# Routing attention followed by a cosine router: first pair prepared in another order, placing steps moved ahead of turns, POOL additions ordered behind DVE additions, scatters split in two

## The chip, the cores and the metric

The kernel runs on one core of a Trainium2 chip. The metric is the device time of one execution in microseconds (us), as the median of several runs. TensorE is called PE here, VectorE DVE, ScalarE ACT, GpSimd POOL and SyncE SP, as the profile calls them.

## The reference

There are two blocks, one behind the other. The first is attention in 4 batches and 8 heads over 768 tokens of 64 numbers. A query sees only the keys that have the same nearest centroid (of 16 in each head). The second block sends each of the 3072 tokens to one of 8 experts.

```python
q_assign = np.argmax(np.einsum('bhsd,hcd->bhsc', q_n, c_n), axis=-1)   # q_n, k_n, c_n: unit rows
k_assign = np.argmax(np.einsum('bhsd,hcd->bhsc', k_n, c_n), axis=-1)
mask = q_assign[:, :, :, None] == k_assign[:, :, None, :]
scores = np.where(mask, scale * (q @ k.T), -1e9)
attn_out = softmax(scores) @ v                      # then (B,H,S,D) -> x of (3072, 512)
logits = (x_n @ emb_n.T) / tau                      # 8 experts
e, gate = argmax(logits), its softmax probability
out[token] = gate * (relu(x[token] @ w1[e]) @ w2[e])     # w1: 512x1024, w2: 1024x512, all float32
```

## The kernel before

All five engines are scheduled by hand (`tc.manual_schedule`): the order of the calls in the Python source is the order of the instructions in the queue of each engine. So a call that is moved in the source is moved in the queues of all the engines that it gives work to. The places and names below are those that the change and the prediction use.

**Attention, 16 pairs.** The work is cut into pairs n of two heads (4 batches of 4 pairs). A pair has two halves of queries (hq 0 and 1) with 6 key blocks each, so 12 units. The main loop takes two units in one turn, so a pair has six turns, it = 0 to 5. In each turn PE computes the scores of two units that come two units later (`scores`, L512: a bfloat16 product with a one-hot table "hot" that adds the mask, and the float32 product of qT and kT), ACT takes the exponential (`expo`, L523, into one of six buffers prob), and PE multiplies two older units by v (`attend`, L534, sum o_ps). DVE adds the probabilities of all blocks of a half into acc (L543 for the first two blocks, L553 for each of the others). Behind the last block of a half ACT copies o_ps to o_sb (L558), and `unite` adds its two parts into o_sum (L567), on POOL for all pairs but the last. `total` (it 0 of the next pair) sums acc over the partitions on PE (L581), DVE turns and inverts the sums (L598, L599), POOL spreads them (L602), `divide` (it 2) applies them (L613, L617), and `rows` turns the result (L634) and writes it to x_rows in memory.

**Preparing a pair.** `turn0` and `turn1` transpose q and k of a pair. From pair 1 on this is done by DVE (L395, one instruction for each), two pairs ahead, in turns 4 and 5. qT and kT have two buffers, so the turn of pair n + 2 has to wait until PE has read those of pair n. For pair 0 PE transposes in halves (L378) and ACT or DVE copies (L384, L386). `products` multiplies with the centroids cnB (PE, L405; DVE turns the result, L414), `choose` finds the nearest centroid (DVE, L423 to L426), `codes` writes its code to cd (ACT, L431, L444), and SP transposes cd by DMA into hot (L449). For pairs from 2 on, products come in turn 0, choose in turn 1 and codes in turn 2 of the pair before. For pair 1 they come in turns 1, 2 and 3.

**begin()** issues the first loads and makes constants. `unit_centroids` scales the centroids (L249, L250, L302), transposes them (L304) and copies them into cnB (L307). It stands between the turns of q and of k. `unit_experts` (L249, L250, L314, L315) is the last call; `turned_experts` (PE L320, DVE L323) comes in turn 2 of pair 0.

**Routing beside the attention.** For three of the four batches the expert choice (`route_pieces`) and the placing of the tokens into blocks (`Places`, table `early`) are DVE, POOL and small PE steps, put into turns of pairs 4 to 15. In the code before, the turns of q and k (it 4 and 5) stand inside `between`, ahead of the route steps and of the table `early`.

**Experts.** After the attention come 4 early items and then 16 items in `later`: block, sized, sized, block, sized, block, ..., sized, block. A block has 128 tokens, a sized item 160 to 272 of one expert. `fetch` gathers rows of x with indirect DMAs from POOL (L1069), `hidden` / `sized_hidden` and `result` / `sized_result` are the two products (L1289, L1305, L1204, L1241), and `send` scatters the pieces of a sized item with 5 to 9 indirect DMAs from POOL (L1080). A block's single scatter (also L1080) stands in `result`. Weights are loaded by SP (L1119).

Of the kernel before, what the change touches and what calls it, by code (L numbers as in the profile page):

```python
# [39 lines left out]
def kernel(  # L40
# [38 lines left out]
    NB = NS + KX  # L79


    MORE = (2, 4, 8)
    NO = sum(MORE)
    assert -(-(N - P - min(CAPS)) // P) <= KX + NO and min(CAPS) >= P
# [92 lines left out]
    def misc():  # L177
        return bank("misc", psM)
# [50 lines left out]
    def keep_up(n, bk):  # L229

        for _ in range(n):
            nc.tensor.matmul(
                bk.rearrange("p (g x) -> p g x", x=P),
                lhsT=onesb,
                rhs=bc(onesb, [P, 4, P], 1),
                start=True,
                stop=True,
            )
# [88 lines left out]
    def begin():  # L327

        nc.scalar.dma_start(out=c_sb, in_=centroids.rearrange("h c d -> (h c) d"))
        load(0, "q")  # L330
        load(0, "k")
        load(0, "v")
        load(1, "qk")
        constants()

        nc.scalar.activation(en_r, epsc[0:E], ACTF.Sqrt)
        norm_rows(cn_r, c_sb, P)
        nc.scalar.dma_start(out=emb, in_=moe_expert_emb)
        nc.scalar.dma_start(out=tau, in_=moe_tau.to_broadcast([E, 1]))
        piece(0, "turn0")  # L340
        unit_centroids()
        piece(0, "turn1")
        norm_rows(en_r, emb, E)

        nc.scalar.activation(cn_r, epsc, ACTF.Exp)
        piece(0, "products")
        for m in range(2):
            scores(m, (1,))
        un[2]["s_ps"] = psO.tile([P, 2, 512], F32, tag="o_ps", name="s_ps2")
        scores(2, (1,))  # L350
        piece(0, "choose")
        piece(0, "codes")
        keep_up(6, misc())
        rest = piece(0, "turn_numbers")
        next(rest)
        for m in range(3):
            scores(m, (0,))
        for m in (0, 2, 1):
            expo(m)
        next(rest, None)  # L360
        token_numbers()
        unit_experts()

    def prep_pieces(n):

# [7 lines left out]
        def turn(nm, half):  # L373
            if half == 0:
                t[nm + "T"] = trp.tile([P, S], F32, tag=nm + "T", name=nm + "T")
            bk = misc() if nm == "k" else idle_ps[:, half]
            for j in range(NJ // 2):
                nc.tensor.transpose(  # L378
                    bk[:, P * j : P * j + P],
                    t[nm][:, NJ // 2 * half + j].rearrange("p h d -> p (h d)"),  # L380
                    ident,
                )
            if nm == "q":
                nc.scalar.copy(t["qT"][:, HS * half : HS * half + HS], bk[:, 0:HS])  # L384
            else:
                (nc.scalar.copy if half else nc.vector.tensor_copy)(  # L386
                    in_halves(t["kT"])[:, half], bk[:, 0:HS].rearrange("p (s t) -> p s t", t=SQ)
                )
# [171 lines left out]
    def unite(g):  # L560

        n, hq, _ = units[GU * g]
        t = ld[n]
        if hq == 0:
            t["o_sum"] = xp.tile([P, 2, HE], F32, tag="o_sum", name="o_sum", bufs=2)
        add = (nc.gpsimd if n + 1 < NP else nc.vector).tensor_tensor
        add(t["o_sum"][:, hq], t["o_sb"][:, 0], t["o_sb"][:, 1], ALU.add)  # L567

# [551 lines left out]
            out=w[:, c], in_=x[ds(e, 1)].rearrange("o (c p) f -> p (o c) f", p=P)[:, c]  # L1120
        )

    def fetch(it):
        mo[it] = {}
        if it.kind == "sized":
            u0, n = FIRST[it.j], WIDE[it.j]
            xs = mo[it]["xs"] = szp.tile([P, max(WIDE), P], F32, tag="xs", name="xs")
            for u in range(n):
                gather(xs[:, u], x_pieces, flat(gpidx)[:, u0 + u : u0 + u + 1], NQ * N)
            return  # L1130
        if it.kind == "whole":
            xin = mo[it]["xin"] = it.xin
            gather(
                xin.rearrange("p w x -> p (w x)"), x_rows, it.tables[1][:, it.col : it.col + 1], N
            )
            return
        xin = mo[it]["xin"] = xip.tile([P, NQ, P], F32, tag="xin", name="xin")
        if it.kind == "early":
            n = SA * P
            gather(  # L1140
                xin.rearrange("p w x -> p (w x)"), x_rows[0:n], gidxs[0][:, it.j : it.j + 1], n
            )
            return
        for w in range(NQ):
            gather(xin[:, w], x_pieces, it.tables[0][:, it.col, w : w + 1], NQ * N)
# [119 lines left out]
            ys[:, 0:n], ys[:, 0:n], bc(flat(gates4)[:, u0 : u0 + n], [P, n, P], 2), ALU.mult  # L1265
        )

    def send(it):

        u0 = FIRST[it.j]  # L1270
        for u in range(WIDE[it.j]):
            at = flat(spidx)[:, u0 + u : u0 + u + 1]
            scatter(out_pieces, at, mo[it]["ys"][:, u], NQ * N)
        del mo[it]

    def flat(t):
        return t.rearrange("p k w -> p (k w)")
# [80 lines left out]
    def between(n, it):  # L1358
        b, nb = divmod(n, NHP)
        if n == 0:  # L1360

            if it == 0:
                piece(1, "turn0")
                piece(1, "turn1")
            elif it == 2:
                piece(1, "choose")
                turned_experts()
            elif it == 3:
                later_constants()
        elif it == 0 and n > 1:  # L1370
            rows(2 * n - 4, 2 * n - 3)
        elif it == 1:
            piece(n + 1, "choose")
        elif it == 3 and n == NP - 1:
            rows(2 * n - 2, 2 * n - 1)
        if it == 4:
            piece(n + 2, "turn0")
        elif it == 5:
            piece(n + 2, "turn1")
        if b > 0:  # L1380
            if nb == 0 and it == 3:
                route[b - 1] = route_pieces(b - 1)
            products, logits, read, norms, choose = route.get(b - 1, (None,) * 5)


            m = NJ * nb + it
            if m in (8, 11, 14):
                read((m - 8) // 3 * 2, (m - 8) // 3 * 2 + 2)
            if m in (15, 16, 18, 19, 21, 22):
                norms((15, 16, 18, 19, 21, 22).index(m))  # L1390
            if (nb, it) == (0, 5):
                logits(0, 1)
            elif (nb, it) == (1, 4):
# [14 lines left out]
        if (n, it) in first:  # L1408
            w, j, i = first[n, it]
            own = E0[j]  # L1410
            if own.e is None:
                own.e = expert_of(own)
            x, chunks = (moe_w1, KD) if w is w1s else (moe_w2, KF)
            load_part(w[own.slot], x, own.e, chunks, i, 2)
# [9 lines left out]
    with tc.manual_schedule(engines=by_hand):  # L1424
        begin()
        for i in range(0, len(units), 2):
# [8 lines left out]
            for m in range(i + 2 if i else 3, min(i + 4, len(units))):  # L1435
                scores(m)
                expo(m)
                if it == (2 if n else 3) and m == i + 2:
                    piece(n + 1, "codes")
            between(n, it)  # L1440
            if it == 4 and n == NP - 1:
# [1 line left out]
            b, nb = divmod(n, NHP)  # L1443
            if (b, nb, it) in early:
                early[b, nb, it]()
            if i + 2 == len(units):
                ats.close()
                tile_waits = {"side": "right", "reuse_waits": "tile"}
                psX = ctx.enter_context(tc.tile_pool(name="psX", bufs=1, space=PSUM, **tile_waits))
                turn_x(E0[0], nc.scalar.copy, xp.tile([P, DM], F32, tag="acc", name="xTm", bufs=3))  # L1450
# [10 lines left out]
                route[b][0](0)  # L1461
            if it == 0 and n > 0:
                total(2 * n - 2, 2 * n - 1)
            if it == (0 if n else 1):
                piece(n + 1, "products")
            if (nb, it) == (0, 4) and b > 0:
                route[b - 1][0](0, 1)
# [70 lines left out]
        pb.hot_gates(NB)  # L1538
        hidden(E0[3])
        weights1(later[1])  # L1540
        fetch(later[1])
        result(E0[2])
        weights2(later[0])
        turn_x(later[0])
        result(E0[3])
# [35 lines left out]
                        more(MORE[0] + MORE[1], MORE[2])  # L1581

        LAST = len(later) - 1
        for i, it in enumerate(later):
            if i == LAST - 1:
                overflow()
# [5 lines left out]
                turn_x(later[i + 1])  # L1592
            if i > 0 and i + 2 < len(later) and later[i + 2].kind == "sized":
                fetch(later[i + 2])
            if i > 0 and later[i - 1].kind == "sized":
                send(later[i - 1])
                if i == LAST:
                    nc.gpsimd.drain()
            if it.kind == "sized":
                sized_hidden(it)  # L1600
            else:
                hidden(it)
            if i == 0:
                pb.gates(slot_gates)
            for j in range(i + 2, min(i + 4, len(later))):
# [62 lines left out]
```

## Time and profile before

| what | value |
|---|---|
| median of 3 runs | 706.15 us (706.08 to 707.62) |
| the profiled execution, its own time | 701.07 us |
| its span, first to last instruction | 699.3 us |
| granted PE clock over the span | 0.999 |
| busy time PE / DVE / ACT / POOL | 686.4 / 385.6 / 263.3 / 253.0 us |
| attention ends, experts begin (on PE) | about 331 us |
| first product with v (L534) of pair 0 | 16.52 us |

The span is what the trace shows; the profiled execution's own time has 1.8 us around it. The profiled execution was 5.1 us shorter than the median of the runs without a profile. In the profile a line "idle before <- releaser" tells how long an engine stood and what ended the wait. Busy PE time is modelled and overlaps between matmuls, so the pace of PE is better read from the distance of equal points in the loop, such as the first L534 of each turn.

### The profile page before, as it was taken

The page shows a single profiled execution, that of the slowest core. Times are in us where ns is not written, and L with a number is a line of the kernel's source. Part 1 is how long each engine was busy: PE and PEld are TensorE (multiplying, and loading weights), DVE is VectorE, ACT ScalarE, POOL GpSimd, SP SyncE. Part 2 cuts the span into 40 slices and gives each one's busy share as a digit, 9 for nine tenths or more (in the row PEclk, how much of TensorE's full clock was granted, in tenths as well). Part 3 has the DMA queues.
Part 4 walks back from the last instruction along what each step waited for, and adds up shares of the span by engine and source line. Part 5 has one row for each costly group of instructions (what it writes and reads, how often), then busy time and mean ns, then how long its engine had stood idle before and what let it go on. Part 6 is the DMA issues. An engine that isn't in the chain of part 4 may idle for free.

```text
span 699.3 us, 16130 instructions
## 1 busy us (share of the span) xinstructions
PE 686.4 (98%) x6517; PEld 461.2 (66%) x6517; DVE 385.6 (55%) x666; ACT 263.3 (38%) x444; POOL 253.0 (36%) x403
## 2 busy tenths in 40 slices
PE   8999999999999999999999999999999999999996
PEld 3544444444444444454966678897979797979694
DVE  5878988998989999999583121240220303030310
ACT  5556564677566765576315110101010111111111
POOL 2122221311133212354214456736264554635402
PEclk9999999999999999999999999999999999999999
DMA  9755567775677678699799978258768686879450
GB/s 135 106 98 100 101 97 96 150 142 106 109 132 151 104 150 155 170 249 256 172 318 355 349 271 281 90 216 290 260 228 301 207 302 233 307 250 323 141 221 32
DMA packets 244156, 135.55 MB, mean 194 GB/s; under 512 B 207840, under 2 KB 207842, under 8 KB 244076
## 3 DMA queue, kind: packets, MB, share of 16 engines
q1 hardware_dynamic: 237084, 121.08, 65.5%
q0 software_dynamic: 6016, 13.12, 5.3%
q8 instruction: 54, 0.88, 0.6%
q10 hardware_dynamic: 976, 0.25, 0.2%
q14 instruction: 26, 0.21, 0.1%
HBM read 115.92 MB, written 13.12 MB: 185 GB/s over the span
## 4 chain that ended last, share of the span: by engine, by line
PE 76%; DVE 7%; issue 6%; DMA 6%; POOL 2%; SPq 1%; ACT 1%; POOLq 0%; DVEq 0%; ACTq 0%
PE s_ps L512 16%; PE o_ps L534 12%; PE h_ps L1289 10%; PE y_ps L1305 10%; PE h_ps L1204 9%; PE y_ps L1241 5%; PE misc L1241 5%; DVE acc L553 3%; DMA out_dram<-ys,spidx 3%; PE x_ps L1204 3%; PE misc L581 2%; PE misc L405 1%; DMA q<-in_q_dram 1%; SPq L212 1%; DMA w1s<-in_moe_w_dram 1%
## 5 line engine op out<-in xcount | busy, mean ns | idle before, releaser
L523 ACT ACTIVATE prob<-s_ps 128x768 f32<-128x768 f32 x192 | 154.2, 814 | 105.4 <-PE s_ps L512 104.4
L512 PE MATMUL s_ps<-qT,kT 64*64 64x384 f32 x1536 | 155.9, 482 | 0.0
L534 PE MATMUL o_ps<-prob,v 64*64 64x385 f32 x1536 | 141.7, 484 | 0.0
L553 DVE TENSOR_TENSOR acc<-acc,prob 128x768 f32<-128x768 f32 x128 | 127.3, 995 | 8.8 <-ACT prob L523 0.5
L534 PEld LDWEIGHTS o_ps<-prob,v 64*64 64x64 f32 x1536 | 59.5, 133 | 63.8 <-issue 56.3
L1250 DVE STREAM_TRANSPOSE ys<-y_ps 128x256 f32<-128x256 f32 (+4 forms) x16 | 6.7, 417 | 153.2 <-PE y_ps L1241 153.2
L567 POOL TENSOR_TENSOR o_sum<-o_sb 128x385 f32<-128x385 f32 x30 | 30.6, 1021 | 161.8 <-ACT o_sb L558 161.8
L1289 PE MATMUL h_ps<-xTm,w1s 128*128 128x128 f32 x768 | 88.3, 275 | 0.0
L1289 PEld LDWEIGHTS h_ps<-xTm,w1s 128*128 128x128 f32 x768 | 87.4, 192 | 1.4 <-issue 1.0
L1305 PE MATMUL y_ps<-w2s,hT 128*128 128x512 f32 x192 | 84.5, 593 | 0.0
L1080 POOL DMA_INDIRECT out_dram<-ys,spidx x56 | 56.5, 1009 | 74.7 <-DVE ys L1264 59.8
L512 PEld LDWEIGHTS s_ps<-qT,kT 64*64 64x64 f32 x1536 | 55.8, 133 | 36.1 <-issue 32.0
L1204 PE MATMUL h_ps<-xTs,w1s 128*128 128x272 f32 (+7 forms) x384 | 72.9, 346 | 1.1 <-ACTq L1565 1.1
L1204 PEld LDWEIGHTS h_ps<-xTs,w1s 128*128 128x128 f32 x384 | 66.6, 190 | 8.0 <-issue 2.4
L1296 ACT ACTIVATE hT<-h_ps 128x512 f32<-128x512 f32 x24 | 14.3, 596 | 144.3 <-PE h_ps L1289 144.3
L512 PE MATMUL s_ps<-hot 64*64 64x384 bf16 x768 | 64.8, 326 | 2.1 <-DMA hot<-cd 0.9
L1069 POOL DMA_INDIRECT xs<-x_rows,gpidx x56 | 57.3, 1023 | 17.1 <-issue 16.8
L1305 PEld LDWEIGHTS y_ps<-w2s,hT 128*128 128x128 f32 x192 | 35.6, 190 | 40.2 <-issue 40.2
L512 PEld LDWEIGHTS <-hot 64*64 64x64 bf16 x768 | 24.3, 106 | 45.6 <-issue 41.9
L602 POOL COPY inv<-inv 32x12 f32<-32x12 f32 x120 | 31.2, 260 | 50.0 <-DVE inv L599 45.6
L1241 PE MATMUL y_ps<-hTs,w2o 128*128 128x272 f32 (+7 forms) x256 | 48.0, 346 | 0.0
L1241 PE MATMUL misc<-hTs,w2o 128*128 128x272 f32 (+7 forms) x256 | 48.0, 346 | 0.0
(270 smaller groups left out, 687.2 us busy)
## 6 DMA issues: line engine op xcount, KB each, us to landing
w1s<-in_moe_w_dram SPq DMA_DIRECT2D x18, 2048.0 KB, 8.3
w2s<-in_moe_w_dram SPq DMA_DIRECT2D x18, 2048.0 KB, 13.2
v<-in_v_dram SPq DMA_DIRECT2D x128, 48.0 KB, 2.4
k<-in_k_dram SPq DMA_DIRECT2D x62, 96.0 KB, 3.6
q<-in_q_dram SPq DMA_DIRECT2D x60, 96.0 KB, 3.6
x_rows<-xb SPq DMA_DIRECT2D x60, 96.0 KB, 2.7
xr<-x_rows SPq DMA_DIRECT2D x9, 512.0 KB, 4.8
w1s<-in_moe_w_dram SPq DMA_DIRECT2D x4, 1024.0 KB, 5.7
```

Source lines behind the costliest of these rows:

```text
L512: nc.tensor.matmul(s_ps[D * half : D * half + D, h, 0:HS], lhsT=l[rows, half], rhs=r[rows], start=part == (1 if len(parts) < 2 else 0), st ...
L523: nc.scalar.activation(d["prob"][:, :, 0:HS], d["s_ps"][:, :, 0:HS], ACTF.Exp, scale=scale)
L534: nc.tensor.matmul(g["o_ps"][D * h : D * h + D, half, 0:HE], lhsT=ld[n]["v"][keys, j, h], rhs=d["prob"][keys, h, 0:HE], start=(j == 0), st ...
L553: nc.vector.tensor_tensor(g["acc"], g["acc"], d["prob"][:, :, 0:HS], ALU.add)
L567: add(t["o_sum"][:, hq], t["o_sb"][:, 0], t["o_sb"][:, 1], ALU.add)
L602: nc.gpsimd.tensor_copy(inv2[M * to : M * to + M, :, i % 2], inv[M * i : M * i + M])
L1069: nc.gpsimd.indirect_dma_start(out=to, out_offset=None, in_=of, in_offset=bass.IndirectOffsetOnAxis(ap=at, axis=0), bounds_check=n - 1, oo ...
L1080: inst = nc.gpsimd.indirect_dma_start(out=to, out_offset=bass.IndirectOffsetOnAxis(ap=at, axis=0), in_=of, in_offset=None, bounds_check=n - 1,
L1204: nc.tensor.matmul(bk, lhsT=w1s[it.slot][:, c, P * f : P * f + P], rhs=d["xT"][:, c, 0:C], start=(c == 0), stop=(c == KD - 1),)
L1241: nc.tensor.matmul(bks[g][:, 0:C], lhsT=d["w2"][:, f, P * g : P * g + P], rhs=d["hT"][:, f, 0:C], start=(f == 0), stop=(f == KF - 1),)
L1289: nc.tensor.matmul(bk[:, m : m + P], lhsT=w1s[it.slot][:, c, f0 + m : f0 + m + P], rhs=d["xT"][:, P * c : P * c + P], start=(c == 0), stop ...
L1305: nc.tensor.matmul(bk, lhsT=d["hT"][:, P * c : P * c + P], rhs=w2s[it.slot][:, c], start=(c == 0), stop=(c == KF - 1),)
```

## The change

- Pair 0: `unit_centroids` is called ahead of the turns of q and k. The transposes of q use two score buffers in place of the two halves of one buffer, and the copy of the second half goes from ACT to DVE. The small loads of the expert embedding and of tau go from ACT's queue to SP's, ahead of the loads of v.
- Pair 1: products, choose and codes come in turns 0, 1 and 2, as for all other pairs. `unit_experts` moves ahead of the copies of the first hot table, and `turned_experts` moves from turn 2 of pair 0 into `begin`, behind the first scores.
- Turns 4 and 5: the turns of q and k of pair n + 2 are issued behind the route steps and behind the table `early`.
- `unite`: a POOL copy of one element of acc is put ahead of the POOL addition, so that the addition waits for the last DVE addition of the half.
- Experts: `fetch` of the first sized item is split in two around `result` of an early item. In each block behind a sized item, but for the last, `send` issues three scatters, and the rest after a POOL copy that waits for the hidden layer of the block.

```diff
+    RUN = 3
@@ begin
         load(0, "q")
         load(0, "k")
+        nc.sync.dma_start(out=emb, in_=moe_expert_emb)
+        nc.sync.dma_start(out=tau, in_=moe_tau.to_broadcast([E, 1]))
         load(0, "v")
...
         norm_rows(cn_r, c_sb, P)
-        nc.scalar.dma_start(out=emb, in_=moe_expert_emb)
-        nc.scalar.dma_start(out=tau, in_=moe_tau.to_broadcast([E, 1]))
+        unit_centroids()
         piece(0, "turn0")
-        unit_centroids()
         piece(0, "turn1")
...
         piece(0, "choose")
         piece(0, "codes")
         keep_up(6, misc())
+        unit_experts()
         rest = piece(0, "turn_numbers")
         next(rest)
         for m in range(3):
             scores(m, (0,))
+        next(rest, None)
+        turned_experts()
         for m in (0, 2, 1):
             expo(m)
-        next(rest, None)
         token_numbers()
-        unit_experts()
@@ turn
-            bk = misc() if nm == "k" else idle_ps[:, half]
+            if nm == "k":
+                bk = misc()
+            else:
+                bk = psS.tile([P, 2, 512], F32, tag="s_ps", name=f"q_ps{half}")[:, 0]
...
-                nc.scalar.copy(t["qT"][:, HS * half : HS * half + HS], bk[:, 0:HS])
+                (nc.vector.tensor_copy if half else nc.scalar.copy)(
+                    t["qT"][:, HS * half : HS * half + HS], bk[:, 0:HS]
+                )
@@ unite
+        if n + 1 < NP:
+            behind = smp.tile([1, 1], F32, tag="behind", name="behind", bufs=1)
+            nc.gpsimd.tensor_copy(behind, gr[g]["acc"][0:1, 1, HS - 1 : HS])
         add = (nc.gpsimd if n + 1 < NP else nc.vector).tensor_tensor
@@ fetch(it, a=0, z=None): a sized item gathers pieces a to z
-            for u in range(n):
+            for u in range(n)[a:z]:
@@ send(it, a=0, z=None)
-        for u in range(WIDE[it.j]):
+        for u in range(n)[a:z]:
...
@@ between
-            elif it == 2:
+            elif it == 1:
                 piece(1, "choose")
-                turned_experts()
...
-        if it == 4:
-            piece(n + 2, "turn0")
-        elif it == 5:
-            piece(n + 2, "turn1")
@@ main loop of the attention
-                if it == (2 if n else 3) and m == i + 2:
+                if it == 2 and m == i + 2:
                     piece(n + 1, "codes")
...
             if (b, nb, it) in early:
                 early[b, nb, it]()
+            if it >= 4:
+                piece(n + 2, f"turn{it - 4}")
...
-            if it == (0 if n else 1):
+            if it == 0:
                 piece(n + 1, "products")
@@ experts
         weights1(later[1])
-        fetch(later[1])
+        fetch(later[1], 0, NQ)
         result(E0[2])
+        fetch(later[1], NQ)
...
+        def wait_hidden(it, f):
+            nc.gpsimd.tensor_copy(pace, mo[it]["hT"][0:1, f : f + 1])
...
+            late = i > 0 and later[i - 1].kind == "sized" and it.kind == "block" and i < LAST
             if i > 0 and later[i - 1].kind == "sized":
-                send(later[i - 1])
+                send(later[i - 1], 0, RUN if late else None)
...
                 hidden(it)
+            if late:
+                wait_hidden(it, F - 1)
+                send(later[i - 1], RUN)
```

More of the change, by code (lines that the diff above doesn't have):

```diff
@@ L1121, in load_part, with fetch @@
         )
-    def fetch(it):
-        mo[it] = {}
+    def fetch(it, a=0, z=None):
+        if a == 0:
+            mo[it] = {}
         if it.kind == "sized":
             u0, n = FIRST[it.j], WIDE[it.j]
-            xs = mo[it]["xs"] = szp.tile([P, max(WIDE), P], F32, tag="xs", name="xs")
-            for u in range(n):
+            if a == 0:
+                mo[it]["xs"] = szp.tile([P, max(WIDE), P], F32, tag="xs", name="xs")
+            xs = mo[it]["xs"]
+            for u in range(n)[a:z]:
                 gather(xs[:, u], x_pieces, flat(gpidx)[:, u0 + u : u0 + u + 1], NQ * N)
@@ L1266, in sized_result, with send @@
         )
-    def send(it):
-        u0 = FIRST[it.j]
-        for u in range(WIDE[it.j]):
+    def send(it, a=0, z=None):
+        u0, n = FIRST[it.j], WIDE[it.j]
+        for u in range(n)[a:z]:
             at = flat(spidx)[:, u0 + u : u0 + u + 1]
             scatter(out_pieces, at, mo[it]["ys"][:, u], NQ * N)
-        del mo[it]
+        if z is None:
+            del mo[it]
     def flat(t):
```

## The prediction

> **What bounds the kernel now.** First the page's busy line, then the busy times by stage, then who PE waited for, in the attention (0 to 330 us) and behind it.
>
> ```profile
> PE 686.4 (98%) x6517; PEld 461.2 (66%) x6517; DVE 385.6 (55%) x666; ACT 263.3 (38%) x444; POOL 253.0 (36%) x403
> ```
> ```profile
> core 0: us, PE busy (x) PEld busy (x) DVE busy (x) ACT busy (x) POOL busy (x), PEclk, DMA share, GB/s
> 14.45:36.77 22.32, 20.87 (x276) 11.72 (x280) 18.77 (x31) 13.84 (x20) 2.83 (x30) 1.00 0.93 113
> 36.77:133.47 96.70, 96.70 (x1357) 46.96 (x1352) 84.29 (x114) 58.95 (x86) 22.41 (x56) 1.00 0.63 104
> 212.21:313.40 101.19, 99.39 (x1366) 48.58 (x1367) 95.86 (x150) 63.81 (x101) 27.82 (x60) 1.00 0.75 162
> ```
> ```profile
> PE misc L581 <- DVE acc L553: 1.6, 2, 1.2
> PE s_ps L512 <- DMA hot<-cd: 0.9, 1, 0.9
> PE s_ps L512 <- ACT prob L523: 0.6, 1, 0.6
> PE idle_ps L378 <- ACT qT L384: 0.6, 1, 0.6
> ```
>
> PE has next to no gaps. What can be won is where its pace is below that of an undisturbed stretch. I take it from the timeline, as the distance of the first L534 of one turn to that of the next. In pairs 1 to 3 a turn takes 2.91, turn 0 4.48 (it holds total and products). Against this, pair 0 has 2.98, 4.52, 2.96, 2.91, 3.98, 2.91, and the losses elsewhere are: pair 6, turn 0: 0.57; pair 9, turn 5: 0.5; turn 0 of pairs 10, 11, 12, 14: 0.44, 0.52, 0.98, 1.70; turn 2 of pair 12: 0.32; turn 1 of pair 14: 0.49. In the third stretch above DVE is busy 95.86 of 101.19 us: there DVE sets the pace. Why, the timeline at the end of pair 11 shows:
>
> ```profile
> 250.78 0.87 POOL L567 TENSOR_TENSOR o_sum<-o_sb 128x385 f32<-128x385 f32 x1 [7.69 <-ACT o_sb L558]
> 251.06 2.47 DVE L553 TENSOR_TENSOR acc<-acc,prob 128x768 f32<-128x768 f32 x2
> 253.58 0.55 PE L581 MATMUL misc<-acc,ones 128*32 128x192 f32 x8 [0.46 <-DVE acc L553]
> ```
>
> Two L553 take 2.01 elsewhere (301.04), here 2.47, because the first met POOL's addition; and PE's total L581 waits for just these. Of the 128 L553, those that meet no POOL work take 0.96; those that start while L567 runs, 1.40 to 1.59. In the third stretch this mean is seen:
>
> ```profile
> L553 DVE TENSOR_TENSOR acc<-acc,prob 128x768 f32<-128x768 f32 x41 | 43.9, 1072 | 3.2 <-ACT prob L523 0.5
> ```
>
> **What the skill says.** The Trainium skill, "SBUF — State Buffer", Who interferes with whom: a DVE instruction with two SBUF inputs and a GpSimd instruction that reads SBUF hold a shared port for the whole instruction, and "issue order, not op shape, decides who blocks". The trace agrees: L553 and L543 (two inputs) stretch, L613 and L634 (one input) take 0.97 with POOL beside them or not. "Perfetto Trace Analysis", Tensor Engine Instruction: ACT, DVE and GpSimd are strict FIFO. It agrees: at 206.14 choose (207.04) stood behind a turn L395 that had waited 0.73 for PE. "DMA: Bandwidth & Descriptors", Anatomy of one DMA: semaphore waits are made by the issuing sequencer before dispatch. SP shows such stands: its v loads go out at 2.98, 4.34, 5.95, though an issue takes 0.3 to 0.5.
>
> **Start, step by step.** Landing times are from the trace's DMA semaphores.
> ```profile
> 6.36 0.55 PE L378 MATMUL idle_ps<-ident,q 128*128 128x128 f32 x3 [0.57 <-ACT qT L384]
> 7.57 0.55 PE L378 MATMUL misc<-ident,k 128*128 128x128 f32 x3 [0.22 <-DVE cnB L307]
> 8.16 0.52 PE L405 MATMUL misc<-qT,cnB 128*32 128x384 f32 x2
> ```
> The centroids are ready at 5.01 (L302), q lands at 5.14: the transpose of the centroids (0.27) costs q at most 0.1. The second half of q then no longer waits for ACT's copy and starts near 5.7, the first half of k (landed 5.93) near 6.0, the second half (landed 6.69) near 6.8 in place of 7.57. So the second copy of kT ends near 7.8 in place of 8.64, and products, choose and codes come 0.8 earlier. unit_experts now stands on DVE ahead of the hot copies: 15.56 to 16.43 before, so 0.87, starting 12.1, ending 13.0, where the copies would be ready at 12.8: 0.2 lost. **The start gains 0.6.** Loads of emb and tau: two SP issues of some 0.5, into the stands between 2.98 and 5.95, so nothing; if that cover fails, the loads of pair 1 (last landed 16.5, needed by its turn at about 16.8) slip by up to 1.1, and PE's products with them. On ACT their 0.8 lay in an idle stretch: nothing gained.
>
> **Pair 0.** turned_experts takes PE from 23.68 to 24.02 now (0.34) and goes into the 0.59 that PE waits for an exponential at 15.72: 0.34 gained. codes one turn earlier, the hot DMA is issued near 24.3 in place of 28.02 and lands 4.2 later, ahead of its use near 30: the extra 1.07 of turn 4 goes. Products in turn 0 need kT of pair 1, turned on DVE by 17.7 (before: 18.25), and PE comes there at 17.3 and has the q half to do first: 0.1 lost. **Pair 0 gains 1.3.**
>
> **The `behind` copy.** A POOL copy of one element has no row; the nearest, pace at L1608, takes 0.18 and up to 0.5 to the next issue. It makes POOL's addition start 0.2 to 0.4 after the half's last L553, so that one is no longer met. Behind the POOL addition stand L602, the cumx additions and later the gathers of the early items; the o_sum that it makes is used half a pair later. It then runs beside L613 or L634 (not blocked) and reaches 0.1 to 0.3 into L617 or L543, which I price at 0.25; bounds 0 and 0.86, a whole hold. Pair 6: DVE waits at turn 0 anyway elsewhere, so all 0.55 comes back. Pair 9 and 10: cumx (POOL to 211.98) holds PE's ranks by 0.15, and turn 0 of pair 10 lost 0.44 to a met L553: 0.55 back, also because choose now stands ahead of the turn and uses its 0.73 of wait. Pairs 11 to 14: DVE has one wait left (0.37 at 226.10), so what counts is its work. Met L553: 0.48, 0.54, 0.45, 0.47, 0.50, 0.62, 0.63 = 3.7, plus the 0.37 that firsts now fills, less 8 x 0.25: 2.1. PE's loss there is 0.52 + 1.30 + 2.19 = 4.0, of which 0.46 is PE work (L978), so 3.5 is the most. **The additions give 0.55 + 0.55 + 2.1 = 3.2**, bounds 0.5 and 4.6.
>
> **Placing ahead of turns** is in these sums; in pairs without such steps nothing moves. A turn delayed by at most 1.2 (firsts) is needed a turn or more later.
>
> **Scatters and gathers.** From 331 on PE waits once, 1.08 at 661.90, at the branch of `overflow`, released by ACT. POOL is busy 135 of 255 us there. Two runs of scatters move 2 to 6 issues of 1.3 behind the hidden layer (7.1) and into the result (6.9): with 8 pieces, the second run ends near the time of the block's own scatter. Next in POOL's queue are gathers used two items later. The split fetch puts one scatter ahead of five gathers, whose last lands 1.3 later, near 400, needed at 406.8. The end is unchanged: the last block is left out. I take 0 (bounds -0.5 and +1).
>
> **Sum.** 0.6 + 1.3 + 3.2 = 5.1, so the profiled 701.07 would be 696.0, and, as the median stood 5.1 above the profile, the median 706.15 becomes 701.0.
>
> **Rivals.** (1) POOL's additions only meet other two-input work (L617, L543, placing steps), and DVE stays as late in pairs 10 to 14: 1.9 and part of 0.55 remain, about 704.0. For it: POOL holds 0.86, and DVE has no free stretch there. Against: a transpose of 0.97 follows each last L553. (2) All of PE's losses come back: 0.6 + 1.3 + 4.6 = 6.5, 699.6; with the start's bounds 698.9. (3) Slower: the first sized item starves. Its last five gathers now stand behind the scatter of E0[2]; DVE's xTs turn waits for them, and the gates for all blocks (L1025) behind that turn on DVE, which PE needs at 406.78. Nothing happens until the last gather lands 5.6 late, near 405.5 (400, then 0.3 for the turn and 0.9 to the gates). If the weight loads beside it (11 us to land) drag it to 414, PE stands 8 us: 709. The landing of 6.6 before speaks against it. (4) The turns stay covered and the waits only change names: 706, no change.
>
> **Numbers.** The likeliest case, 4 to 6 gained: 0.52. Rival 1 (1.0 to 3.5 gained): 0.26. Rival 2: 0.10. Rival 4: 0.06. Slower, rival 3 and unnamed: 0.06. A measurement can tell about 0.3% (2.1 us) from no change. Rival 1 lies across that bound, two thirds of it beyond. So faster 0.79, same 0.15, slower 0.06. Range 698.9 to 704.6: from rival 2 to where only the start and part of the rest remain.
>
> **What would show it.** L405 of pair 0 near 7.3; first L534 near 15.9 in place of 16.52; turn 4 of pair 0 at 2.9 and pair 1 starting near 34.9 (36.77 now); L553 with a maximum near 1.0; turn 0 near 4.5 in pairs 6 and 10 to 12. The step for DVE is wrong if L543 and L617 grow by as much as L553 shrinks; the whole is wrong if PE gets new waits behind 331 us.

## The result, and the profile after

The median after is **700.27 us** (six runs, 699.54 to 701.63), against 706.07 us before (six runs). The ratio is **0.9918, 95% interval 0.9906 to 0.9929**: 5.8 us shorter. The forecast was 701.0 (698.9 to 704.6). The profiled execution took 699.54 us with a span of 697.7, only 1.53 less than the 701.07 of the profile before. So this pair of profiles shows less than the medians do, and why must be answered as well.

First the page's busy line, then the stretches that answer to those shown of before: pair 0 (with the same 276 matmuls), pairs 1 to 5, pairs 10 to 14, and then, as a fourth, the experts from their first hidden product to the last matmul.

```profile
PE 684.7 (98%) x6517; PEld 459.1 (66%) x6517; DVE 381.4 (55%) x667; ACT 261.5 (37%) x443; POOL 252.7 (36%) x439
```
```profile
core 0: us, PE busy (x) PEld busy (x) DVE busy (x) ACT busy (x) POOL busy (x), PEclk, DMA share, GB/s
14.10:34.77 20.67, 20.42 (x276) 10.11 (x272) 16.16 (x25) 13.58 (x20) 3.01 (x30) 1.00 0.83 125
34.77:131.47 96.70, 96.70 (x1357) 46.96 (x1352) 85.81 (x117) 58.96 (x86) 24.25 (x66) 1.00 0.62 105
209.43:306.86 97.43, 97.43 (x1367) 47.75 (x1367) 92.42 (x151) 63.92 (x101) 26.94 (x70) 1.00 0.74 171
324.77:692.12 367.35, 362.68 (x2118) 303.03 (x2114) 92.44 (x234) 55.08 (x123) 165.73 (x179) 1.00 0.71 244
```

The third stretch was 101.19 with PE busy for 99.39; now it is 97.43 and PE is busy for all of it, with DVE at 92.42 (95.86 before). The stretch of pairs 1 to 5 has its old 96.70. The experts begin at 324.77 in place of 331.18: the attention is **6.41 us** shorter. But the same experts took 362.39 before and 367.35 here, so 4.96 of it is lost again. The experts of before in the same columns:

```profile
331.18:693.57 362.39, 361.31 (x2118) 303.07 (x2114) 93.04 (x234) 56.12 (x123) 165.18 (x173) 1.00 0.72 248
```

Who PE waited for in the kernel after, over the whole span, shows where most of the 4.96 went:

```profile
PE x_ps L1217 <- ACT hTs L1224: 2.1, 1, 2.1
PE h_ps L1303 <- issue: 1.2, 3, 0.5
PE h_ps L1217 <- ACTq L1577: 1.1, 1, 1.1
...
PE s_ps L519 <- DVE hot L478: 0.7, 1, 0.7
```

The wait of 1.6 for acc, and those for the hot DMA and for ACT's qT, are gone. The two first lines are new and lie in the experts; the third stands in the profile of before too (1.08, under another line number). (L519, L541, L560 and L591 are the L512, L534, L553 and L581 of before.)

The start, and the end of pair 11 at the point shown of before, in the timeline of after:

```profile
5.17 0.30 PE L305 MATMUL misc<-ident,cn 128*128 128x128 f32 x1 [0.39 <-POOL gate_p L275]
5.33 0.85 PE L383 MATMUL q_ps<-ident,q 128*128 128x128 f32 x6
6.12 0.52 PE L383 MATMUL misc<-ident,k 128*128 128x128 f32 x3
6.89 0.52 PE L383 MATMUL misc<-ident,k 128*128 128x128 f32 x3 [0.25 <-DVE qT L389]
7.38 0.52 PE L412 MATMUL misc<-qT,cnB 128*32 128x384 f32 x2
```
```profile
246.47 1.98 DVE L560 TENSOR_TENSOR acc<-acc,prob 128x768 f32<-128x768 f32 x2
...
248.37 0.97 DVE L644 STREAM_TRANSPOSE xb<-xT 128x768 f32<-128x768 f32 x1
248.59 0.18 POOL L575 COPY behind<-acc 1x1 f32<-1x1 f32 x1 [8.26 <-DVE acc L560]
248.73 0.85 POOL L577 TENSOR_TENSOR o_sum<-o_sb 128x385 f32<-128x385 f32 x1
...
248.94 0.88 PE L591 MATMUL misc<-acc,ones 128*32 128x192 f32 x16
```

All six transposes of q run as one group, and products begin at 7.38 in place of 8.16. At the end of pair 11 POOL's addition waits for the last addition of DVE and then runs beside a transpose; the two L560 take 1.98 (2.47 before) and PE's total is whole (before it was cut, with 0.46 of waiting inside). Over the whole kernel, first before, then after:

```profile
L553 DVE TENSOR_TENSOR acc<-acc,prob 128x768 f32<-128x768 f32 x128 | 127.3, 995 | 8.8 <-ACT prob L523 0.5
L560 DVE TENSOR_TENSOR acc<-acc,prob 128x768 f32<-128x768 f32 x128 | 121.6, 950 | 8.5
L575 POOL COPY behind<-acc 1x1 f32<-1x1 f32 x30 | 6.7, 223 | 177.9 <-DVE acc L560 169.1
```

Ten of the 128 additions had 1.40 to 1.59 before; now the longest is one of 1.18, which was there before too, and no other exceeds 1.02. DVE's additions give 5.7 us back (127.3 to 121.6) for 6.7 us of copies on POOL, which has the time; POOL's own additions also shrink, from 30.6 to 26.6 us.

The pace, as distances in us of the first product with v of each turn, which are free of modelled ends:

| place | before | after | change |
|---|---|---|---|
| first product with v | 16.52 | 16.03 | -0.49 |
| pair 0 | 20.25 | 18.75 | -1.50 |
| pair 6, turn 0 | 5.06 | 4.49 | -0.57 |
| pair 9, turn 5 / pair 10, turn 0 | 3.41 / 4.92 | 3.20 / 4.54 | -0.59 |
| turn 0 of pairs 11, 12, 14 | 5.00, 5.46, 6.18 | 4.48, 4.49, 4.49 | -3.18 |
| pair 12, turn 2 / pair 14, turn 1 | 3.23 / 3.40 | 3.01 / 3.39 | -0.23 |
| pair 15 | 17.78 | 17.91 | +0.13 |

The column adds to -6.43; the experts' start shows -6.41. The first two rows are those of this pair of profiles. In all traces, the first product comes at 16.50 to 17.24 in the four with the old start and at 15.94 to 16.40 in the ten with the new one, 0.58 apart in the mean; pair 0 takes 19.60 to 20.26 in the four and 18.74 or 18.75 in the ten.

### The profile page after: what moved, and what is told of

It reads as the page before. It is cut to its first block, busy times and chain, and to the rows that moved or that the text cites. A ratio compares the mean times of both kernels' runs of the same rounds, so it can differ in the third digit from the quotient of the medians.

```text
span 697.7 us, 16185 instructions
## 1 busy us (share of the span) xinstructions
PE 684.7 (98%) x6517; PEld 459.1 (66%) x6517; DVE 381.4 (55%) x667; ACT 261.5 (37%) x443; POOL 252.7 (36%) x439
## 4 chain that ended last, share of the span: by engine, by line
PE 89%; issue 4%; DMA 3%; POOL 1%; DVE 1%; another core or an unknown queue 1%; POOLq 0%; ACT 0%; DVEq 0%
PE s_ps L519 22%; PE o_ps L541 18%; PE h_ps L1303 10%; PE y_ps L1319 10%; PE h_ps L1217 9%; PE y_ps L1254 5%; PE misc L1254 5%; PE x_ps L1217 3%; DMA out_dram<-ys,spidx 3%; PE misc L591 2%; PE misc L412 2%; PE misc L670 1%; POOL out_dram L1090 0%; POOL xin L1079 0%
## 5 line engine op out<-in xcount | busy, mean ns | idle before, releaser
L519 PE MATMUL s_ps<-qT,kT 64*64 64x384 f32 x1536 | 155.6, 482 | 0.0
L541 PE MATMUL o_ps<-prob,v 64*64 64x385 f32 x1536 | 141.2, 483 | 0.0
L560 DVE TENSOR_TENSOR acc<-acc,prob 128x768 f32<-128x768 f32 x128 | 121.6, 950 | 8.5
L541 PEld LDWEIGHTS o_ps<-prob,v 64*64 64x64 f32 x1536 | 58.4, 133 | 65.0 <-issue 57.8
L519 PEld LDWEIGHTS s_ps<-qT,kT 64*64 64x64 f32 x1536 | 55.2, 133 | 36.9 <-issue 32.3
L575 POOL COPY behind<-acc 1x1 f32<-1x1 f32 x30 | 6.7, 223 | 177.9 <-DVE acc L560 169.1
L519 PE MATMUL s_ps<-hot 64*64 64x384 bf16 x768 | 64.2, 325 | 1.0 <-DVE hot L478 0.7
L519 PEld LDWEIGHTS <-hot 64*64 64x64 bf16 x768 | 23.8, 106 | 43.8 <-issue 41.8
L1254 PEld LDWEIGHTS y_ps<-hTs,w2o 128*128 128x128 f32 x256 | 44.4, 190 | 2.9 <-issue 0.4
```

The source lines that it names most:

```text
L519: nc.tensor.matmul(s_ps[D * half : D * half + D, h, 0:HS], lhsT=l[rows, half], rhs=r[rows], start=part == (1 if len(parts) < 2 else 0), st ...
L541: nc.tensor.matmul(g["o_ps"][D * h : D * h + D, half, 0:HE], lhsT=ld[n]["v"][keys, j, h], rhs=d["prob"][keys, h, 0:HE], start=(j == 0), st ...
L560: nc.vector.tensor_tensor(g["acc"], g["acc"], d["prob"][:, :, 0:HS], ALU.add)
L1254: nc.tensor.matmul(bks[g][:, 0:C], lhsT=d["w2"][:, f, P * g : P * g + P], rhs=d["hT"][:, f, 0:C], start=(f == 0), stop=(f == KF - 1),)
```

## The experiments

The runs were made in three groups, each on one chip with runs of before beside them: e1 to e4 (median of before 705.74), e5 to e8 (703.42), e9 to e12 (701.44). Ratios are to before within the group; a gain in us is the difference of the medians. The expectations of the last two groups build on the runs ahead of them. Two questions were open: which edit wins what in the attention, and whether the scatters and gathers cause the stands in the experts.

**The start alone (e3)**: before, with the new order of pair 0 and 1, and with the moved loads and constants.

```diff
+        nc.sync.dma_start(out=emb, in_=moe_expert_emb)
+        nc.sync.dma_start(out=tau, in_=moe_tau.to_broadcast([E, 1]))
...
+        unit_centroids()
         piece(0, "turn0")
-        unit_centroids()
...
+            elif it == 1:
                 piece(1, "choose")
```

> The kernel before with the new order of the first pair and of pair 1 alone (centroids ahead of q, q in two score buffers, unit_experts and turned_experts early, products in turn 0). Theory 1: 1.9 to 2.0 us faster than before; pair 1 starts near 34.8 in its trace, and the losses in turn 0 of pairs 6, 10 to 12 and 14 stay as before. Rival (DVE is as late in pairs 10 to 14 whatever comes before and gives it back): under 0.7 us faster.

Measured: 703.88 us, ratio 0.9973 (0.9965 to 0.9981), 1.9 us. Pair 1 starts at 35.06 (36.77 before, 34.77 after), and from there to the experts it takes 294.34, as before does (294.41). The first theory holds: the start and pair 0 are worth about 2, and nothing of it is lost or multiplied later. The run tests these edits together; which of them wins what is read from the traces alone.

**Without the copy (e4), and the copy alone (e6).**

```diff
 # e4: after, without
-            behind = smp.tile([1, 1], F32, tag="behind", name="behind", bufs=1)
-            nc.gpsimd.tensor_copy(behind, gr[g]["acc"][0:1, 1, HS - 1 : HS])
 # e6: before, with just these two lines
```

> The changed kernel without the POOL copy that holds the addition of unite back, all else changed. Theory 1 (the addition that meets an L553 sets the loss): about 2.5 to 3.5 us faster than before, so some 2.5 to 3.5 of the 5.8 gone; L553 again up to 1.6 us in the trace and turn 0 of pairs 11, 12 and 14 again longer than 4.5 by 0.3 to 1.5. Rival (placing ahead of turns is what gave pairs 9 to 14 their time): less than 1 of the 5.8 gone, turn 0 near 4.5.

Measured: 703.18 us, ratio 0.9963 (0.9950 to 0.9976). The experts begin at 327.09, 2.3 later than in after. Turn 0 of pairs 6, 10 and 11 keeps its 4.48, 4.55 and 4.49; pairs 12 and 14 fall back to 5.45 and 5.73, and turn 2 of pair 12 to 3.23. So the first theory is right in the size (2.6 us faster than before) and in pairs 12 and 14, and wrong for pair 11. The median itself tells little: the executions spread from 700.62 to 706.72, and the traced one has the longest experts of all (368.29). PE's waits between 100 and 327 us in e4:

```profile
PE misc L588 <- DVE acc L560: 1.2, 2, 0.7
...
```

This is the line of before (1.6), on PE's total again. In after the same view, from 100 us to the end of the attention, has no line at all.

> The kernel before with the POOL copy ahead of unite's addition alone. The run without this copy left pairs 6, 10 and 11 without a loss, so the order of the turns alone is enough there. Theory 2 (in pairs 6, 10 and 11 either of the two is enough, in pairs 12 and 14 the copy is needed): turn 0 of pairs 6, 10, 11, 12, 14 near 4.5 each, and 3 to 4 us faster than before. Theory 1 (as in the prediction, the copy alone frees pair 6 and most of 10 to 14): 2.5 to 3.2 us faster. Rival (without the order of the turns the addition is only late elsewhere): under 1.5 us faster.

Measured: 699.07 us, ratio 0.9937 (0.9923 to 0.9950). Turn 0 of pairs 6, 11, 12 and 14 is 4.49, 4.52, 4.64 and 4.49, but turn 5 of pair 9 has its 3.41, turn 0 of pair 10 its 4.88, and turn 2 of pair 12 is 3.45, even longer than before (3.23). So the copy alone frees most places, and leaves those of pairs 9 and 10 and turn 2 of pair 12. The theories are both missed: the gain of 4.4 is above either, and pair 10 is not freed. The trace shows 3.2 of gain behind the start of pair 1. That execution started 0.7 late (16.52 to 17.24), so only distances behind pair 1 are used.

**Without the order of the turns (e9)**: after, with the turns of q and k ahead of the placing steps again.

```diff
+        if it == 4:
+            piece(n + 2, "turn0")
+        elif it == 5:
+            piece(n + 2, "turn1")
...
-            if it >= 4:
-                piece(n + 2, f"turn{it - 4}")
```

> After with the turns of q and k put back ahead of the route steps and of the table of early placings (pairs 2 on); all else as after. Theory 1 (either the POOL copy or the order frees pairs 6 and 11; pairs 9 and 10 need the order): turn 0 of pair 6 about 4.5, of pair 10 about 4.9 (0.4 more than after), turn 5 of pair 9 about 3.4 (0.2 more), pairs 12 and 14 at most 0.3 longer; the experts begin 0.6 to 1.0 later than in after, near 325.5, and the time is 0.6 to 1.0 longer than after's: a ratio to before near 0.991 on a chip where after has 0.990. Rival (copy and order add up, each carrying about half of the 4.4): the experts begin 2 or more later, and the ratio is near 0.993.

Measured: 695.56 us, ratio 0.9918 (0.9905 to 0.9932), against 694.79 for after (e12) beside it: 0.77 longer, and 1.04 longer from pair 1 to the experts (290.90 against 289.86). Pair 9 has 3.41 and pair 10 4.80 as in e6; pair 12 has 4.65 and 3.45, so turn 2 of pair 12 was underestimated in the expectation (0.44 here). Otherwise the first theory holds. PE's waits in e9 from 100 us to the end of the attention:

```profile
PE s_ps L519 <- ACT prob L530: 0.4, 1, 0.4
PE misc L806 <- POOL cumx L724: 0.2, 1, 0.2
```

The second stands in pair 9, turn 5: PE's step of the placing waits for POOL's running counts, cumx. They follow DVE's route steps, which stood behind a turn of q that had waited 0.72 for PE. The copy does nothing for that. The 16 products with v behind that wait then take 1.78 in place of 1.52, for a reason that the trace doesn't show; that is 0.26 of pair 10's loss. The first wait is in turn 2 of pair 12. ACT's exponential stands behind `codes` there, and `codes` starts just as DVE's `choose` ends, 0.88 behind the start of the turn (0.45 in after).

The time from the start of pair 1 to the experts puts copy and order side by side:

| | turns ahead of placing | turns behind placing |
|---|---|---|
| no copy | 294.41 (before), 294.34 (e3) | 292.34 (e4) |
| copy | 291.16 (e6), 290.90 (e9) | 290.00 (after), 289.86 (e12), 289.80 (e11) |

The copy alone is worth 3.2, the order alone 2.1, both together 4.4: less than the sum by 0.9. Pairs 6 and 11 (0.57 and 0.52) are freed by either, and so is 0.45 of pair 14; against that, 0.6 of pair 12 comes back only with both.

What decides turn 0 is how late DVE is: how long behind the first product with v of a pair DVE ends its last addition for the pair before it, which PE's total needs. In each cell stands this lateness, then the length of turn 0:

| pair | before | order alone (e4) | copy alone (e6) | after |
|---|---|---|---|---|
| 6 | 1.91, 5.06 | 0.46, 4.48 | 1.28, 4.49 | 0.46, 4.49 |
| 11 | 1.86, 5.00 | 1.25, 4.49 | 1.38, 4.52 | 0.70, 4.48 |
| 12 | 2.31, 5.46 | 2.31, 5.45 | 1.50, 4.64 | 0.91, 4.49 |
| 14 | 3.03, 6.18 | 2.59, 5.73 | 1.28, 4.49 | 1.06, 4.49 |

In pairs 6 and 11 to 14 of all traces turn 0 is 4.48 to 4.49 while the lateness is at most 1.28; from 1.37 on it is longer by just what exceeds 1.34. So a place is free once DVE is early enough, even where an addition is still met: in e4 the addition that ends pair 10 takes 1.52, and pair 11 loses nothing.

The timeline of pair 5 and 6 shows how the order does it. In before:

```profile
127.90 0.98 DVE L395 STREAM_TRANSPOSE qT<-q 128x768 f32<-128x768 f32 x1 [0.73 <-PE s_ps L512]
...
129.94 2.02 DVE L553 TENSOR_TENSOR acc<-acc,prob 128x768 f32<-128x768 f32 x2
129.98 3.76 POOL L714 TENSOR_TENSOR cumx<-cumx,eq 128x8 bf16<-128x8 bf16 x6 [4.50 <-DVE eq L712]
131.87 0.97 DVE L395 STREAM_TRANSPOSE kT<-k 128x768 f32<-128x768 f32 x1
132.77 2.61 DVE L553 TENSOR_TENSOR acc<-acc,prob 128x768 f32<-128x768 f32 x2
133.71 0.86 POOL L567 TENSOR_TENSOR o_sum<-o_sb 128x385 f32<-128x385 f32 x1
```

And in e4, the order without the copy:

```profile
126.29 0.97 DVE L402 STREAM_TRANSPOSE qT<-q 128x768 f32<-128x768 f32 x1
126.33 3.17 POOL L721 TENSOR_TENSOR cumx<-cumx,eq 128x8 bf16<-128x8 bf16 x6 [2.82 <-DVE eq L719]
...
129.98 1.98 DVE L560 TENSOR_TENSOR acc<-acc,prob 128x768 f32<-128x768 f32 x2
131.06 1.62 POOL L574 TENSOR_TENSOR o_sum<-o_sb 128x385 f32<-128x385 f32 x1 [1.56 <-ACT o_sb L565]
```

Before, DVE stood 0.73 at the turn of q, since PE was still reading the old qT, with the route steps queued behind it. In e4 the route steps fill that wait. DVE's last addition then ends 19.49 behind the start of pair 5 (131.96 less 112.47) in place of 20.94 (135.38 less 114.44). The two additions still overlap, but their order has turned. Before, POOL's starts at 133.71 and DVE's second one at 133.79: DVE's takes 1.59. In e4 DVE's starts at 131.00 and POOL's at 131.06: DVE's keeps its 0.96, and POOL's takes 1.62 in place of 0.86. For PE this doesn't matter here: with a stretch of 0.63 DVE would still end 1.09 behind the start of pair 6, within the 1.34. The copy alone leaves it at 1.28, so only just within.

**The scatters and gathers: without them (e1, and again e11), alone (e2), and only the scatters in one run (e8).**

```diff
 # e1, e11: after, with
-        fetch(later[1], 0, NQ)
+        fetch(later[1])
-        fetch(later[1], NQ)
-            late = i > 0 and later[i - 1].kind == "sized" and it.kind == "block" and i < LAST
+            late = False
 # e8: after, with late = False only.  e2: before, with fetch and send as in after
```

> The changed kernel without the split of scatters and of the gather (fetch and send as before), all else changed. Theory 1 (the gain is won in the attention, the runs of scatters are worth nothing): about 5.8 us faster than before, as the whole change, within 0.7; in its trace PE enters the experts at about 324.8. Rival A (the runs of scatters win something in the experts): 1.5 us or more of the 5.8 is gone. Rival B (they cost the 5 us by which the experts were longer in the trace of the changed kernel than in that of before): 9 to 11 us faster than before, and no PE waits between 331 and 650.

Measured: 698.75 us, ratio 0.9903 (0.9885 to 0.9922): 7.0 faster, with the experts from 324.74. So the runs of scatters don't win 1.5 (rival A), and don't cost what rival B says: 9 isn't reached, and PE has three waits of 0.3 to 0.8 between 331 and 650. But 7.0 is above the first theory's range too, and after itself was not run on that chip.

> The kernel before with the split of scatters and gather alone. Theory 1: within 0.7 us of before. Rival A: faster by 1.5 us or more. Rival B: slower by 3 to 5 us. In all of them the attention in its trace is that of before (experts entered at about 331).

Measured: 706.42 us, ratio 1.0022 (1.0003 to 1.0041), the attention as before: 0.7 slower by the medians, 1.5 by the ratio, whose interval is just off one. Five of the 14 executions, all those above 708 us, have a granted clock of 0.994 to 0.997; the nine at 0.998 to 1.000 have a median of 705.15, against 705.74 for before. So the run shows no cost of the split.

> The changed kernel with all scatters of a sized item sent in one run again, but the gather of the first sized item still split in two. Theory A (the second run of scatters joins the block's scatter and the next gathers to one long burst of indirect DMAs on POOL, beside which PE's releases of ACT come late): 6.5 to 7.3 us faster than before, as the run without both splits. Theory B (the split gather costs): as the changed kernel, 5.3 to 6 us faster.

Measured: 695.99 us, ratio 0.9895 (0.9880 to 0.9910), against after beside it:

> The changed kernel, unchanged, beside the next run on the same chip. 5.3 to 6 us faster than before.

Measured: 696.38 us, ratio 0.9898 (0.9883 to 0.9913). The two can't be told apart; both are 7.0 to 7.4 faster than before, so neither theory can be told from the size alone.

> After without the two runs of scatters and without the split fetch, now beside after on one chip. If the two runs cost what before with them alone showed (ratio 1.0022): 1 to 1.5 us shorter than after, a ratio to before lower by 0.0015 to 0.002. If they are worth nothing: the two ratios agree within 0.001.

Measured: 694.52 us, ratio 0.9904 (0.9889 to 0.9919), against after:

> After unchanged, as the yardstick for the other kernels on this chip: a ratio to before of 0.990 to 0.992; experts begin 6 us earlier than in before.

Measured: 694.79 us, ratio 0.9907 (0.9892 to 0.9922). The 0.27 between e11 and e12 lies ahead of the experts in their traces: the first product with v came at 15.94 and 16.35, and the experts took 362.42 and 362.41. So on this chip **the split is worth nothing**, as forecast, and the version without it is as fast as after and simpler.

**Are POOL's DMAs the cause of the stands? (e5 and e10)** e5 is before, unchanged, for one more profile of it.

> The kernel before, unchanged, profiled again. In the traces of the changed kernel and of the four experiments, PE stands 2 to 5 us between 331 and 655 us and ACT's Relu comes up to 7 us behind the matmul that it waits for; the first trace of the kernel before has none of this. Theory 1 (the first trace was a lucky execution, and these waits are in most executions of either kernel): this trace has them too, a span of 702 to 705 and the same attention (pair 1 at about 36.8, experts at about 331). Rival (the change brings these waits): no such waits, a span near 699.3.

Measured: 702.69 us. The attention is as in the first profile (experts from 330.98), but the experts took 364.2, with waits of PE of 1.0 in all and 0.4 at the longest, and Relus that start up to 3.2 behind the modelled end of their product. The span, 700.9, is below the expected 702 to 705. So **before has the stands too**, and the change isn't what brings them. On the same chip after's experts take as long (364.0 in e7), so it doesn't lengthen them there. e10 is e1 with only the first scatter of each sized item (8 in place of 56; the other rows of the sized items are left out):

```diff
-        for u in range(n)[a:z]:
+        for u in range(n)[a:z][0:1]:
```

> After without the two runs of scatters and without the split fetch, and with only the first scatter of each sized item: most rows of the sized items are left out of the result. Theory 2 (bursts of POOL's indirect DMAs make ACT's releases late and PE stand in the experts): the stands of PE of 1 to 4 us between 331 and 655 go, the experts take about 362.4 from their first hidden product to PE's end (that of the first profile of before), and the time is 1.5 to 4 us below that of no_runs. Rival (the late releases have another cause, such as the weight loads): stands of 1 us and more stay, the length stays at 364 to 366, and the time is within 1 us of no_runs.

Measured: 694.79 us, ratio 0.9906 (0.9891 to 0.9922), the experts 362.42, no stand. It would fit the theory, but e9, e11 and e12 with all their scatters have 362.42, 362.42 and 362.41 and no stand either. So the run tells nothing of the cause: on this chip there was nothing to take away. It does show that 48 scatters of 1.0 us on POOL cost no time where PE isn't held.

What the stands look like is seen on ACT, in one sized item. After, in its first profile:

```profile
475.37 0.37 ACT L1224 ACTIVATE hTs<-h_ps 128x240 f32<-128x240 f32 x1 [0.99 <-issue]
478.82 0.37 ACT L1224 ACTIVATE hTs<-h_ps 128x240 f32<-128x240 f32 x1 [3.08 <-PE h_ps L1217]
482.42 0.37 ACT L1224 ACTIVATE hTs<-h_ps 128x240 f32<-128x240 f32 x1 [3.23 <-PE h_ps L1217]
486.70 0.37 ACT L1224 ACTIVATE hTs<-x_ps 128x240 f32<-128x240 f32 x1 [3.91 <-remote]
486.97 0.63 ACT L1224 ACTIVATE hTs<-h_ps 128x240 f32<-128x240 f32 x2
```

The same program and item in e12:

```profile
473.71 0.37 ACT L1224 ACTIVATE hTs<-h_ps 128x240 f32<-128x240 f32 x1 [0.99 <-PE h_ps L1217]
475.27 0.37 ACT L1224 ACTIVATE hTs<-h_ps 128x240 f32<-128x240 f32 x1 [1.19 <-PE h_ps L1217]
476.89 0.37 ACT L1224 ACTIVATE hTs<-h_ps 128x240 f32<-128x240 f32 x1 [1.25 <-PE h_ps L1217]
478.51 0.37 ACT L1224 ACTIVATE hTs<-x_ps 128x240 f32<-128x240 f32 x1 [1.25 <-PE x_ps L1217]
```

In e12 a Relu comes every 1.62 us, as PE finishes its chunks. In after they come 3.4 to 4.3 apart and then bunched, though PE's matmuls start at an even pitch: the Relu of 486.70 starts 6.9 us behind the start of the last matmul that it waits for (479.76; the median of this distance is 0.4), until PE has no buffer left and stands 2.1. The semaphore event that releases it comes at 486.68. Since the ends of matmuls are modelled, the trace can't tell a late signal from a product that was finished late. The experts took 362.4 in the first profile of before and in e9 to e12, 364 in e5 to e8, 367.4 in the first profile of after, and 365.7 to 368.3 in e1 to e4, whatever the edit. So the term goes with the chip and the time of the run, which the runs can't part. Its cause stays open; the weight loads, which the expectation of e10 names, were not tested.

## Why the prediction was right

**The time.** 701.0 was forecast, 700.27 measured: a gain of 5.8 where the sum had 5.1. The same pair of kernels gave 7.0 on the chip of e7 and 6.65 on that of e12 (701.44 to 694.79), the one group of which no trace has stands. Both lie beyond the likeliest case (4 to 6 gained), near rival 2's 6.5, and the attention is 6.4 shorter. So the mechanism was right and the sum too small, and that the first median came within 0.7 of the forecast is partly luck: in those runs part of the gain did not show, for a reason that isn't known.

**Start, 0.6**: 0.49 here. Products came at 7.38 (forecast 7.3) and the first product with v at 16.03 (15.9). The means of the traces are 0.58 apart (above), and products come at 7.37 to 8.22 with the new start, so nothing finer can be read from one pair. The loads of emb and tau cost SP nothing, as forecast: the first q of pair 1 is issued at 8.78 (8.73 before). The transposes of q start at 5.33 in place of 5.28, within the 0.1 allowed.

**Pair 0, 1.3**: 1.50. The hot DMA is issued at 24.17 (24.3 forecast), turn 4 is 2.91 as forecast, and pair 1 starts at 34.77 (34.9). The loss of 0.1 allowed for kT of pair 1 did not show.

**Pairs 6, 9 and 10, 0.55 each**: 0.57 and 0.59. The sizes were right, the reasons partly not. I gave pair 6 to the addition that is no longer met; e6 confirms that, but e4 frees it without the copy. In pair 10 I named both; e6 and e9 show that the order is needed, the copy alone leaving 0.3 to 0.4 there, and e9's wait for cumx is the one I had named. (What I called choose at 207.04 is the expert choice of `route_pieces`, L708, not the `choose` of a pair.)

**Pairs 11 to 14, 2.1**: 3.41, and this is **the term that was mis-sized**. I took 3.7 of shortened additions plus 0.37 of filled wait, and then subtracted 8 x 0.25 because POOL's addition would reach into L543 or L617. (The 3.7 lists seven additions, so eight charges were one too many; with seven the term is 2.3.) That price wasn't paid, as these lines of 200 to 310 us show, before and then after:

```profile
L553 DVE TENSOR_TENSOR acc<-acc,prob 128x768 f32<-128x768 f32 x44 | 46.8, 1063 | 2.9
L543 DVE SCALAR_TENSOR_TENSOR acc<-prob,prob 128x768 f32<-128x768 f32 x11 | 10.4, 947 | 0.0
L617 DVE SCALAR_TENSOR_TENSOR xT<-o_sum,den 128x768 f32<-128x768 f32 x6 | 6.2, 1026 | 0.2
```
```profile
L560 DVE TENSOR_TENSOR acc<-acc,prob 128x768 f32<-128x768 f32 x44 | 41.7, 949 | 2.9
L550 DVE SCALAR_TENSOR_TENSOR acc<-prob,prob 128x768 f32<-128x768 f32 x12 | 11.3, 945 | 0.0
L627 DVE SCALAR_TENSOR_TENSOR xT<-o_sum,den 128x768 f32<-128x768 f32 x6 | 6.2, 1035 | 0.2
```

The mean of the 44 additions falls from 1063 to 949 ns, so by 5.0 us in all; those of the two other lines go from 947 to 945 and from 1026 to 1035. The step from work to time was off as well. I took PE's gain as the work that DVE saves, but PE loses only what DVE's lateness exceeds 1.34, and after has at most 1.06. So nearly all of the 3.5 that PE had lost comes back, and the rest is slack on DVE. This is rival 2's mechanism; it had 4.6 for the additions, and 4.41 is what pairs 1 to 15 show. Rival 1 is refuted: in it L543 and L617 would have grown as L553 shrinks.

The Trainium skill, "SBUF — State Buffer", Who interferes with whom, carried this step: which of two such instructions is issued first decides which one waits. e4 and e6 agree with it. With the same shapes on both engines, POOL's addition behind DVE's last addition removes the stretches of 1.40 to 1.59 (e6), and where DVE is first by 0.06, POOL's is the one that is stretched (e4). The copy guards the last addition of a half only: of the nine traces with it, e1 has one of 1.74, an addition of the next half.

**Scatters and gathers, 0**: right: e11 and e12 are 0.3 us apart, and e7 and e8, where only the split of the scatters differs, 0.4. Rival 3 (a starving first sized item) did not come: its hidden product starts 75.8 behind that of the experts, in before (406.99 less 331.18) and in e12 (400.75 less 324.95).

**From profile to median.** I added 5.1 to the sum because the first profile of before stood that far below its median, without a reason for it. For the profile itself the sum said 696.0, and 699.54 came. A likely reason is now seen: the first profile of before had no stands (experts 362.39), while every profile of e1 to e8, one of before among them, has them. How long the experts were in the runs behind that median isn't on record. The prediction's sign of failure, new waits of PE behind 331 us, did appear in the profile after, and e5 shows it without the change.

## What to carry to other kernels

Where an instruction of a helper engine stretches an urgent one, as POOL's addition did here, put it behind the urgent one with a tiny dependent copy: 0.22 us on POOL took 0.4 to 0.6 off each addition that was met. To price it, look for the slack: here DVE's lateness cost PE nothing up to 1.34, and one for one beyond it. Before pricing what such a shift collides with, look at what runs in its new place; and when two remedies act at the same place, count the place once, and look for places that need both. When a profile and a median disagree, compare the same stage across several profiles of the unchanged kernel before putting the difference down to the change.

## What was unexpected in the hardware

- The same program takes 701.4, 703.4, 705.7 and 706.1 us in the four sets of runs, at a granted PE clock of 0.997 to 1.0 in all profiles; in the traces most of the difference lies in the experts (362.4 to 368.3), where ACT's Relus start up to 6.9 us behind the start of their last matmul. In e12, which has no stands, none of 88 is later than 1.43.
- The late ones come in bunches: at 486.7 to 487.6 in after three Relus run back to back that were due 1.6 apart.
- Which of two overlapping additions is stretched turned on 0.06 to 0.08 us: POOL's first, and DVE's takes 1.59 (before); DVE's first, and POOL's takes 1.62 (e4).
